# One core: whole 64-row weights ahead of the second third, the band's last quarter by GpSimd, and the loads of x5 to x9 released one by one

## The chip, the cores and the metric

The kernel runs on one core of a Trainium2 chip. The metric is the device time of one execution in microseconds. The core has TensorE (PE) for products, VectorE (DVE), ScalarE (ACT), GpSimd (POOL) and SyncE (SP), which in this kernel issues nearly all DMA transfers; in the profile "SPq" is the queue of SP.

## The reference

Per batch (8) and position (4160) a causal convolution of width 7 is taken, with one softmax-normalised set of 7 weights for each of 8 heads of 24 columns, and its result goes through a feed-forward layer with three products and a maximum.

```python
w = softmax(weight, axis=-1)                       # 8 heads x 7
out = np.einsum('hk,bskhg->bshg', w, x_unf)        # x padded by 6 rows in front
x = out.reshape(B * S, D)                          # 33280 x 192
h = np.maximum(np.maximum(x @ w1, x @ w2), x @ w3) # 192 -> 768
return (h @ w_out).astype(np.float32)              # 768 -> 192
```

## The kernel before

The 33280 rows are cut into 65 blocks of 512 (`NBLK`). All products are in 16 bits. The maximum is taken as max(x(w1-w3), x(w2-w3), 0) + x w3: `make_wd` (L320) subtracts w3 from w1 and w2, the columns' 192 rows being held as 128 rows (n = 0 and 1) and 64 rows of both (n = 2, w1 in partitions 0 to 63, w2 in 64 to 127), `top` (L508, L509) takes the maximum with ScalarE's relu and VectorE's maximum, and x w3 w_out is added with a small matrix m.

The order of the work on every engine is the order of the program; nothing is rearranged. Each engine runs its own list and waits for the others by semaphores. SP's list holds loads, stores (L684) and transposes (L429) in program order, and a transfer that waits holds up all behind it. A transfer also waits for the one eight places earlier to land, since there are eight DMA semaphores in turn.

The start: SP loads x0 and x1 (`load_x`, L167), then a third of the 128-row weights (`load_wa`, L229), the 64 rows of w3 (L244), the 64 rows of w1 and w2 for the first third of the columns (`load_wb`, L233), the second third of the 128 rows, the remaining two thirds of the 64 rows, the last third of the 128 rows, w_out, x2, x3. Meanwhile the band matrix of the convolution is built: products with shifted weights (L291) into two PSUM tiles, columns 0 to 27 and 28 to 37 of a window, from where ScalarE and VectorE copy it to four quarters of 32 partitions (L299), heads 5 to 7 first and heads 0 to 4 later. `cast_dense` (L216) turns x0 to x3 into 16 bits, and `conv_dense` (L396) multiplies them with the band; block 0's half with heads 5 to 7 goes first (`order=(1, 0)`). `l1_dense` (L544) computes the first layer of blocks 0 and 1 in parts of 128 rows ("F") and 64 rows ("H").

From block 4 on the convolution goes another way: x is loaded in halves of 39 rows by 8 pieces, GpSimd casts it (`cast_x`, L199), `conv` (L375) multiplies it, `evac` (L415) copies the result, `turn` (L429) issues two DMA transposes, and `double` (L438) lets GpSimd copy each half of the partitions to the other. The first layer (`l1`, L521) of a block reads that result. In the main loop over t, block t's first layer is interleaved with the second layer of block t-1 (`st2`, L585), the result of t-2 is stored, and the convolution of a later block stands in the middle: block 4's in block 2, 5 and 6's in block 3, 7 and 8's in block 4, and so on.

The loads of x4 to x6 stand in one piece ahead of block 0's third and fourth tile. x7 is loaded after blocks 0 and 1 are done, x8 and x9 within block 2. A load of x4 or later waits until the zeroing of its buffer (`zero_x`, L137 or L140) or the last reader of the buffer is done.

Of the kernel before, what the change touches and what calls it, by code (L numbers as in the profile page):

```python
# [15 lines left out]
P = 128  # L16
KW = 7
PAD = KW - 1
NHEAD = 8
# [4 lines left out]
HALF = P // 2  # L24
WIN = 32 + PAD
# [3 lines left out]
def kernel(  # L29
# [12 lines left out]
    nc = tc.nc  # L42
    ctx.enter_context(tc.manual_schedule())

    B, SEQ, D = x.shape
    H, KWs = weight.shape
    assert H == NHEAD and KWs == KW and D == GRP * NHEAD
    DFF = moe_w1.shape[1]
# [9 lines left out]
    for b in range(B):  # L58
        s = nfull * NBLK
        while s < SEQ:  # L60
            n = min(SEQ - s, NBLK - off)
# [24 lines left out]
    NDENSE = 4  # L86
    chunks_of = [conv_chunks(blk) for blk in blocks[:NDENSE]]
    NQ = len(chunks_of[0])
    TOK = 32
# [29 lines left out]
    xin, xbuf, XBUF, loaded = {}, [], 7, set()  # L119
# [11 lines left out]
    def zero_x(t, q0=0, q1=NR, eng=None):  # L131
# [4 lines left out]
        if eng is not None:  # L136
# [4 lines left out]
                       in_=bass.AP(tensor=zero.tensor, offset=zero.offset,  # L141
                                   ap=[list(zero.ap[0]), [0, q1 - q0], [1, D]]))

    def load_x(t, eng=nc.sync):
        if not 0 <= t < NB:
            return
        loaded.add(t)
        get_x(t)
        xf = xin[t][0]
        if t < NDENSE:  # L150
            todo = [(0, c[3], c[1] * SEQ + c[2], i) for i, c in enumerate(chunks_of[t])]
        else:
            todo = [(HALF * (i // NR) + (0 if s else LAP), KR if s else TOK,
                     b * SEQ + s - (LAP if s else 0), i % NR) for i, (b, s) in enumerate(rows_of(t))]
        parts = []
        i, n = 0, len(todo)
        row = [c[2] for c in todo]
        while i < n:
            k = i
            while k + 1 < n and todo[k + 1][:2] == todo[i][:2] and row[k + 1] - row[k] == row[i + 1] - row[i]:  # L160
                k += 1
            step = row[i + 1] - row[i] if k > i else 0
            p0, rlen, _, q0 = todo[i]
            q1 = todo[k][3] + 1
            src = bass.AP(tensor=x.tensor, offset=row[i] * D,
                          ap=[[D, rlen], [step * D, q1 - q0], [1, D]])
            eng.dma_start(out=xf[p0:p0 + rlen, q0:q1, :], in_=src)  # L167
            if parts and parts[-1][0] == rlen:
                parts[-1] = (rlen, parts[-1][1], q1)
            else:  # L170
                parts.append((rlen, q0, q1))
            i = k + 1
        xin[t] = [xf, todo[0][0], parts]
# [30 lines left out]
    xz = {t: [const.tile([P, NQ, D], FP16, name=f"xz_{t}_{v}") for v in range(2)] for t in range(2)}  # L204
    xz[2], xz[3] = xz[0], xz[1]

    def cast_dense(t, copies, slots_=range(CYC // 32), keep=False):
        xf, _, parts = xin[t] if keep else xin.pop(t)
        for v, copy in enumerate(copies):
            if copy is None:  # L210
                continue
            for s in slots_:
                cut = GRP * (32 * s // GRP + 1)
                a, b = (32 * s, cut) if v == 0 else (cut, 32 * s + 32)
                for (rl, q0, q1) in parts:
                    copy(  # L216
                        out=xz[t][v][0:rl, q0:q1, :].rearrange("p q (k c) -> p q k c", c=CYC)[:, :, :, a:b],
                        in_=xf[0:rl, q0:q1, :].rearrange("p q (k c) -> p q k c", c=CYC)[:, :, :, a:b])
# [6 lines left out]
    PW = 2 * P  # L225
# [2 lines left out]
        for st, n, wsrc in ((w3s, 0, moe_w3), (ws, 0, moe_w1), (ws, 1, moe_w2)):  # L228
            nc.sync.dma_start(out=st[:, n, f], in_=wsrc[0:P, f])  # L229

    def load_wb(f):
        for st, lo, n, wsrc in ((ws, 0, 2, moe_w1), (ws, HALF, 2, moe_w2)):
            nc.sync.dma_start(out=st[lo:lo + HALF, n, f], in_=wsrc[P:D, f])  # L233

    wk = const.tile([NHEAD, SMALL], FP32, name="wk")[:, 0:KW]
    nc.scalar.dma_start(out=wk[:], in_=weight)
# [4 lines left out]
    load_x(0)  # L241
    load_x(1)
    load_wa(slice(0, PW))
    nc.sync.dma_start(out=w3s[0:HALF, 1, :], in_=moe_w3[P:D, :])  # L244
    load_wb(slice(0, PW))
    for t in range(2, NDENSE):
        get_x(t)
    ident = const.tile([P, P], FP32)
# [32 lines left out]
    nc.vector.reciprocal(out=wrec[:], in_=wrec[:])  # L281
    zero_x(4)
    nc.vector.tensor_scalar_mul(out=line[0:NHEAD, 31:31 + KW], in0=wexp[:, 0:KW], scalar1=wrec[:])
    cast_dense(0, (nc.vector.tensor_copy, nc.gpsimd.tensor_copy), (1, 2), keep=True)
    CUT = 28
    bands_ = []
    for lo, hi, copy in ((0, CUT, nc.scalar.copy), (CUT, WIN, nc.vector.tensor_copy)):
# [5 lines left out]
                             rhs=ident16[:, 0:4 * NHEAD], start=True, stop=True)  # L293
        bands_.append((lo, hi, copy, bps))
    keep_warm((NBLK, NBLK, P), psp, "p")
    for h0, h1 in ((5, NHEAD), (0, 5)):
        for lo, hi, copy, bps in bands_:
            for a in range(4):
                copy(out=band[32 * a:32 * a + 32, h0:h1, 32 * a + lo:32 * a + hi],  # L299
                     in_=bps[:, 0:hi - lo, h0:h1].rearrange("p c h -> p h c"))  # L300
        if h0:
            cast_dense(0, (nc.vector.tensor_copy, nc.gpsimd.tensor_copy), (0,))
    load_wa(slice(PW, 2 * PW))
    load_wb(slice(PW, DFF))
    load_wa(slice(2 * PW, DFF))
    nc.sync.dma_start(out=wos[:], in_=moe_w_out.rearrange("(j p) c -> p j c", p=P))
    load_x(2)
# [76 lines left out]
    def conv_dense(t, copies, pools=((None, None),) * 2, order=(0, 1)):  # L384


        yd = dense[t] = ydp.tile([P, NC, NBLK], FP16, tag="yd", name=f"yd_{t}")
        for n in order:
            slots_ = ((0, 1, 2, 3), (4, 5, 4, 5))[n]
            pool, tag = pools[n]  # L390
            ps = (pool or psw).tile([P, NBLK], FP32, tag=tag or "w", name=f"D{n}_{t}")
            for (q, b, row_lo, rlen, lo, hi, cc) in chunks_of[t]:
                for v in range(2):
                    for g, s in enumerate(slots_):
                        h = (32 * s + 31 * v) // GRP
                        nc.tensor.matmul(  # L396
                            ps[32 * g:32 * g + 32, lo:hi],
                            lhsT=xz[t][v][0:rlen, q, 32 * s:32 * s + 32],
                            rhs=band[0:rlen, h, cc:cc + hi - lo],
                            start=(v == 0), stop=(v == 1), tile_position=(0, 32 * g))  # L400
            copies[n](out=yd[:, 2 * n, :], in_=ps[:])
# [96 lines left out]
    def meet():  # L498

        emit(True)  # L500
        assert not ops
        clock[0] = clock[1] = 0
# [189 lines left out]
    WPWQ = ((psw, "w"), (psp, "p"), (psw, "w"), (psq, "q"))  # L692
    ACT, DVE = nc.scalar.copy, nc.vector.tensor_copy
    GP = nc.gpsimd.tensor_copy
    conv_dense(0, (ACT, ACT), order=(1, 0))
    cast_dense(1, (DVE, GP), (1, 2, 0))
    zero_x(5, eng=nc.gpsimd)
    make_wd(0, 0, 2)
# [14 lines left out]
    l1_dense([(1, 0, WW), (1, 1, WW)], "HF")  # L713
    tops((1, 0), (1, 1))
    zero_x(6)
    for t in range(NDENSE, XBUF):
        load_x(t)
    l1_dense([(0, 2, PQ), (0, 3, PQ)], "FH")
    tops((0, 2), (0, 3))
    l1_dense([(1, 2, WW), (1, 3, WW)], "HF")  # L720
# [10 lines left out]
    first_hidden(0)  # L731
    first_hidden(1)
    conv_dense(2, (ACT, DVE), (WW[0], PQ[1]))
    cast_x(4)
    cross(2, ACT, DVE)
    make_m(0)
# [1 line left out]
    zero_x(0, NQ)  # L738
    zero_x(2, NQ, NR, nc.vector)
    zero_x(3, NQ, NR, nc.vector)  # L740
    load_x(7)
    cast_x(5)

    convs_at = {2: 4, 3: 5, 4: 7}
# [16 lines left out]
    for t in range(2, NB):  # L763
        u = convs_at.get(t, NB)
        late = t > 2 and u < NB
        if t in (3, 4):
            double(t + 1)
        if t > 3:
            for v in range(casts.get(t - 1, 8) + 1, casts[t] + 1):
                cast_x(v)  # L770
        l1(t, 0)
        if t == 2:
            first_rest()
        elif t == 3:
            cast_x(8)
            nc.gpsimd.tensor_copy(out=m16[0:HALF, 2, :], in_=m16[HALF:P, 0, :])
            nc.gpsimd.tensor_copy(out=m16[HALF:P, 2, :], in_=m16[HALF:P, 1, :])
        if t > 3 and not late:
            op(lambda t=t: (store(t - 2, 0, 4, (nc.sync,)),
                            turn(t + 2, (2,)) if place(t + 2)[1:] in ((0, 4), (0, 5)) else None,  # L780
                            turn(t + 1, (4,)) if place(t + 1)[1:] == (0, 5) else None, load_on(t)))
        else:
            op(lambda t=t: store(t - 2, 0, 4, (nc.sync,)))
        cuts = ROOM if late else EVEN
        st2(t - 1, (cuts[0], cuts[0]))
        for j in range(1, NJ):
            l1(t, j)
            if late and j == 1:
                st2(t - 1, (cuts[0] + OWN + AHEAD, cuts[0] + OWN))
                meet()  # L790
                quad, second = u >= QUADS, u < QUADS or t == u - 3
                conv(u, WPWQ, range(4 * second, 4 * second + 4) if quad else range(NHEAD))
                for i in (0, 2):
                    evac(u, i)
                for i in (1, 3):
                    evac(u, i, nc.vector.tensor_copy)
                if second:
                    turn(u)
                load_on(t)
            if t == 2 and j == 1:  # L800
                meet()
                conv_dense(3, (ACT, DVE))
                zero_x(1, NQ, NR, nc.vector)
                cross(3, GP, GP)
                load_x(8)
                cast_x(6)
            elif t == 2 and j == 3:
                meet()
                conv(u, WW)
                evac(u, 0)  # L810
                evac(u, 1, nc.vector.tensor_copy)
                turn(4)
                load_x(9)
                cast_x(7)
            st2(t - 1, (cuts[j], cuts[j]))
            if j == 1 and t > 4 and t + 2 in pairs and pairs[t + 2][1] % 2 == 0:
                double(t + 2)
            if t == NB - 1 and j == 3:
                op(lambda: store(NB - 2, 0, 2, (nc.sync,)))
        if t == NB - 1:  # L820
            op(lambda: store(NB - 2, 2, 4, (nc.sync,)))
# [29 lines left out]
```

## Time and profile before

| | |
|---|---|
| median of 3 runs | 454.19 us (453.32 to 454.22) |
| profiled execution | 454.16 us, its span 452.4 us |
| granted TensorE clock | 1.00 |
| TensorE busy | 445.5 us, 98% |
| VectorE, ScalarE, GpSimd busy | 354.6, 320.2, 207.6 us |
| TensorE's waits, 0 to 110 us / from 60 us | 3.8 us / none listed |
| DMA | 72.01 MB, mean 159 GB/s |

The page gives busy time by engine and the chain that ended last. A list of waits gives, for each engine and line, who ended the idle time, with the total, the number and the longest in microseconds. A timeline row gives start, duration, engine, line, operation and, in brackets, the idle time before it and what ended it. Matmul ends are modelled, and a busy TensorE is not TensorE at its peak.

### The profile page before, as it was taken

The page shows a single profiled execution, that of the slowest core. Times are in us where ns is not written, and L with a number is a line of the kernel's source. Part 1 is how long each engine was busy: PE and PEld are TensorE (multiplying, and loading weights), DVE is VectorE, ACT ScalarE, POOL GpSimd, SP SyncE. Part 2 cuts the span into 40 slices and gives each one's busy share as a digit, 9 for nine tenths or more (in the row PEclk, how much of TensorE's full clock was granted, in tenths as well). Part 3 has the DMA queues.
Part 4 walks back from the last instruction along what each step waited for, and adds up shares of the span by engine and source line. Part 5 has one row for each costly group of instructions (what it writes and reads, how often), then busy time and mean ns, then how long its engine had stood idle before and what let it go on. Part 6 is the DMA issues. An engine that isn't in the chain of part 4 may idle for free.

```text
span 452.4 us, 18264 instructions
## 1 busy us (share of the span) xinstructions
PE 445.5 (98%) x7576; PEld 409.8 (91%) x7576; DVE 354.6 (78%) x607; ACT 320.2 (71%) x601; POOL 207.6 (46%) x239
## 2 busy tenths in 40 slices
PE   7999999999999999999999999999999999999997
PEld 4469999999999989999999999999999999999996
DVE  6668787878878787787887787887887887887775
ACT  6967767767777677676676776777776776776664
POOL 5864836556463533724824635525533644224000
PEclk9999999999999999999999999999999999999999
DMA  7968987696885659649649748657649668152123
GB/s 197 239 181 167 203 186 197 155 217 171 170 220 147 165 137 205 162 121 199 167 127 198 178 110 191 191 114 193 178 112 197 172 157 143 54 136 75 58 71 106
DMA packets 128163, 72.01 MB, mean 159 GB/s; under 512 B 52305, under 2 KB 127888, under 8 KB 128080
## 3 DMA queue, kind: packets, MB, share of 16 engines
q1 hardware_dynamic: 127919, 70.75, 65.9%
q8 instruction: 59, 0.97, 0.9%
q14 instruction: 25, 0.20, 0.2%
q10 hardware_dynamic: 160, 0.10, 0.1%
HBM read 33.28 MB, written 25.56 MB: 130 GB/s over the span
## 4 chain that ended last, share of the span: by engine, by line
PE 96%; DMA 1%; ACT 1%; SPq 1%; issue 1%; DVE 0%; ACTq 0%
PE po L585 36%; PE lq L521 32%; PE lp L521 22%; PE G L375 3%; DMA wall<-in_moe_w_dram 1%; ACT r L508 1%; PE D L396 1%; PE po L643 0%; PE po L616 0%; PE lw L544 0%; SPq L229 0%; SPq L167 0%; PE pm L355 0%; ACT wall L324 0%; PE lq L544 0%
## 5 line engine op out<-in xcount | busy, mean ns | idle before, releaser
L585 PE MATMUL po<-wo,h 64*128 64x192 f16 x3024 | 331.7, 243 | 0.0
L509 DVE TENSOR_TENSOR h<-r,lq 128x512 f16<-128x512 f16 x384 | 263.0, 686 | 86.2 <-ACT r L508 76.3
L508 ACT ACTIVATE r<-lp 128x512 f16<-128x512 f32 x384 | 228.9, 597 | 113.8 <-PE lp L521 103.0
L521 PE MATMUL lp<-yp,wd 64*128 64x512 f16 x1098 | 295.6, 376 | 0.0
L521 PE MATMUL lq<-yp,wd 64*128 64x512 f16 x1098 | 295.5, 376 | 0.0
L585 PEld LDWEIGHTS <-h 64*128 64x128 f16 x3024 | 242.7, 94 | 5.4 <-issue 4.1
L521 PEld LDWEIGHTS <-wd 64*128 64x128 f16 x2268 | 181.7, 94 | 14.8 <-issue 0.2
L199 POOL CAST x<-xf 103x768 f16<-103x768 f32 x122 | 97.3, 825 | 114.4 <-DMA xf<-in_x_dram 99.6
L585 PE MATMUL po<-m,yp 64*128 64x192 f16 x720 | 140.3, 243 | 0.0
L438 POOL COPY yp<-yp 64x1536 f16<-64x1536 f16 (+1 forms) x70 | 90.9, 1298 | 86.0 <-DMA yp<-ys 49.1
L593 DVE TENSOR_TENSOR o<-a,po 128x384 f32<-128x384 f32 x126 | 69.0, 547 | 0.0
L585 PEld LDWEIGHTS <-yp 64*128 64x128 f16 x720 | 66.3, 94 | 0.1
L592 ACT COPY a<-po 128x384 f32<-128x384 f32 x126 | 59.6, 473 | 0.0
L415 ACT CAST ys<-G 128x480 f16<-128x480 f32 (+1 forms) x53 | 25.4, 530 | 9.5 <-PE G L375 9.2
L415 DVE CAST ys<-G 128x480 f16<-128x480 f32 (+1 forms) x53 | 30.1, 610 | 0.0
L375 PE MATMUL G<-x,band 39*32 39x240 f16 (+3 forms) x1024 | 16.5, 242 | 0.0
L375 PEld LDWEIGHTS <-band 39*32 39x32 f16 x1024 | 10.2, 92 | 4.6 <-issue 4.1
L521 PE MATMUL lq<-yd,wd 64*128 64x512 f16 x36 | 9.7, 376 | 0.0
L521 PE MATMUL lp<-yd,wd 64*128 64x512 f16 x36 | 9.7, 376 | 0.0
L544 PEld LDWEIGHTS <-wd 128*128 128x128 f16 (+1 forms) x48 | 3.0, 95 | 7.3 <-issue 1.7
L396 PEld LDWEIGHTS <-xz 112*32 112x32 f16 x320 | 4.1, 96 | 2.9 <-issue 1.4
L216 POOL CAST xz<-xf 112x160 f16<-112x160 f32 (+2 forms) x18 | 5.1, 328 | 3.2 <-DMA xf<-in_x_dram 3.0
(75 smaller groups left out, 100.0 us busy)
## 6 DMA issues: line engine op xcount, KB each, us to landing
xf<-in_x_dram SPq DMA_DIRECT2D x113, 234.0 KB
out_dram<-o SPq DMA_DIRECT2D x62, 384.0 KB
xf<-in_x_dram SPq DMA_DIRECT2D x7, 204.8 KB
wall<-in_moe_w_dram SPq DMA_DIRECT2D x11, 128.0 KB
xf<-in_x_dram SPq DMA_DIRECT2D x3, 420.0 KB
yp<-ys SPq DMA_TRANSPOSE x70
out_dram<-o SPq DMA_DIRECT2D x5, 192.0 KB
wos<-in_moe_w_out_dram SPq DMA_DIRECT2D x1, 576.0 KB
```

The costliest lines, as they stand in the source:

```text
L199: nc.gpsimd.tensor_copy(out=x16s[t0][0:K, :, :, u, r, :].rearrange("p h j c -> p j h c"), in_=xf[0:K, 4 * r:4 * r + 4, :].rearrange("p j ( ...
L216: copy(out=xz[t][v][0:rl, q0:q1, :].rearrange("p q (k c) -> p q k c", c=CYC)[:, :, :, a:b], in_=xf[0:rl, q0:q1, :].rearrange("p q (k c) -> ...
L375: nc.tensor.matmul(G[2 * (k // per) + i][TOK * j:TOK * (j + 1), k % per, :], lhsT=band[row, h, HALF * i + LAP:HALF * i + KR], rhs=x16s[t0] ...
L396: nc.tensor.matmul(ps[32 * g:32 * g + 32, lo:hi], lhsT=xz[t][v][0:rlen, q, 32 * s:32 * s + 32], rhs=band[0:rlen, h, cc:cc + hi - lo], star ...
L415: copy(out=slots[t][:, i % 2, :, :, GRP * h0:GRP * (h0 + per)].rearrange("p u r (h c) -> p h (u r) c", c=GRP), in_=G[i][:].rearrange("p h ...
L438: nc.gpsimd.tensor_copy(out=yp[HALF * i:HALF * (i + 1), 1, :, :, :, :].rearrange("p i u k n -> p (i u k n)"), in_=yp[HALF * (1 - i):HALF * ...
L508: nc.scalar.activation(out=r[:], in_=ps[0][:], func=AF.Relu)
L509: nc.vector.tensor_max(out=hs[t][:, j, :], in0=r[:], in1=ps[1][:])
L521: nc.tensor.matmul(ps[i][:], lhsT=w_of(i, c, j), rhs=y_all(t, i, c), start=(n == 0), stop=(n == NC - 1))
L585: nc.tensor.matmul(ps[b0, i][:, s % 2, :], lhsT=a, rhs=b, start=first, stop=last)
L592: nc.scalar.copy(out=a[:], in_=ps[s - 1, 0][:])
L593: nc.vector.tensor_add(out=outs[t][:, s - 1:s + 1, :], in0=a[:], in1=ps[s - 1, 1][:])
```

## The change

Three things are altered.

1. `load_wb` now loads the 64 rows of w3, w1 and w2 each whole (192 KB), ahead of the second third of the 128-row weights. The piece-wise loads of w1 and w2 are gone.
2. The band is copied for all heads at once, by ScalarE and VectorE for three quarters of the partitions; the fourth is copied by GpSimd from the first. x0's cast is done in one go ahead of it, and block 0's convolution takes its halves in the plain order.
3. `release_x(t)` writes one element of x_t's buffer with VectorE and then issues the load, so that the load waits for VectorE to come to that place in its list. x4 is loaded where x4 to x6 were; x5 is released after block 2's convolution, x6 ahead of block 3's, x7 after the evacuation of block 4's convolution, x8 behind the fifth step of block 2 and x9 behind the first step of block 3. The casts of x5 to x8 follow later in GpSimd's list.

```diff
+    def release_x(t):
+
+        get_x(t)
+        nc.vector.memset(xin[t][0][TOK:TOK + 1, 0, 0:1], 0.0)
+        load_x(t)
...
-    def load_wb(f):
-        for st, lo, n, wsrc in ((ws, 0, 2, moe_w1), (ws, HALF, 2, moe_w2)):
-            nc.sync.dma_start(out=st[lo:lo + HALF, n, f], in_=wsrc[P:D, f])
+    def load_wb():
+        for st, lo, n, wsrc in ((w3s, 0, 1, moe_w3), (ws, 0, 2, moe_w1), (ws, HALF, 2, moe_w2)):
+            nc.sync.dma_start(out=st[lo:lo + HALF, n, :], in_=wsrc[P:D, :])
...
     load_wa(slice(0, PW))
-    nc.sync.dma_start(out=w3s[0:HALF, 1, :], in_=moe_w3[P:D, :])
-    load_wb(slice(0, PW))
+    load_wb()
...
-    cast_dense(0, (nc.vector.tensor_copy, nc.gpsimd.tensor_copy), (1, 2), keep=True)
+    cast_dense(0, (nc.vector.tensor_copy, nc.gpsimd.tensor_copy))
...
-    for h0, h1 in ((5, NHEAD), (0, 5)):
-        for lo, hi, copy, bps in bands_:
-            for a in range(4):
-                copy(out=band[32 * a:32 * a + 32, h0:h1, 32 * a + lo:32 * a + hi],
-                     in_=bps[:, 0:hi - lo, h0:h1].rearrange("p c h -> p h c"))
-        if h0:
-            cast_dense(0, (nc.vector.tensor_copy, nc.gpsimd.tensor_copy), (0,))
+    for lo, hi, copy, bps in bands_:
+        for a in range(3):
+            copy(out=band[32 * a:32 * a + 32, :, 32 * a + lo:32 * a + hi],
+                 in_=bps[:, 0:hi - lo, :].rearrange("p c h -> p h c"))
+    nc.gpsimd.tensor_copy(out=band[96:P, :, 96:96 + WIN], in_=band[0:32, :, 0:WIN])
     load_wa(slice(PW, 2 * PW))
-    load_wb(slice(PW, DFF))
     load_wa(slice(2 * PW, DFF))
...
-    conv_dense(0, (ACT, ACT), order=(1, 0))
+    conv_dense(0, (ACT, ACT))
...
-    for t in range(NDENSE, XBUF):
-        load_x(t)
+    load_x(4)
...
     conv_dense(2, (ACT, DVE), (WW[0], PQ[1]))
+    release_x(5)
     cast_x(4)
...
-    load_x(7)
-    cast_x(5)
...
         elif t == 3:
-            cast_x(8)
+            release_x(9)
+            cast_x(7)
...
             if t == 2 and j == 1:
                 meet()
+                release_x(6)
                 conv_dense(3, (ACT, DVE))
                 zero_x(1, NQ, NR, nc.vector)
                 cross(3, GP, GP)
-                load_x(8)
-                cast_x(6)
+                cast_x(5)
             elif t == 2 and j == 3:
...
                 turn(4)
-                load_x(9)
-                cast_x(7)
+                release_x(7)
+                cast_x(6)
+            elif t == 2 and j == 5:
+                release_x(8)
+            if t == 3 and j == 3:
+                cast_x(8)
```

More of the change, by code (lines that the diff above doesn't have):

```diff
@@ L205, with cast_dense @@
     xz[2], xz[3] = xz[0], xz[1]
-    def cast_dense(t, copies, slots_=range(CYC // 32), keep=False):
-        xf, _, parts = xin[t] if keep else xin.pop(t)
+    def cast_dense(t, copies, slots_=range(CYC // 32)):
+        xf, _, parts = xin.pop(t)
         for v, copy in enumerate(copies):
```

## The prediction

> **What bounds the kernel now.** First the busy shares and the shares of the chain that ended last, from the page.
>
> ```profile
> span 452.4 us, 18264 instructions
> ...
> PE 445.5 (98%) x7576; PEld 409.8 (91%) x7576; DVE 354.6 (78%) x607; ACT 320.2 (71%) x601; POOL 207.6 (46%) x239
> ...
> PE 96%; DMA 1%; ACT 1%; SPq 1%; issue 1%; DVE 0%; ACTq 0%
> ```
>
> TensorE is the chain for 96%. Nothing that keeps it busy is touched, so the change is worth what it adds to or takes from TensorE's waits. The list of TensorE's waits in the first 110 us has them all; from 60 us on the same list is empty.
>
> ```profile
> PE idle L260 <- DVE idle L255: 1.2, 1, 1.2
> PE lp L544 <- DVE wd L320: 1.1, 1, 1.1
> PE D L396 <- issue: 0.8, 1, 0.8
> PE D L396 <- ACT band L299: 0.5, 1, 0.5
> ```
>
> The second and the third are the ones that the change can move. The chain in order of time says what they hang on.
>
> ```profile
> 3.71 6.13 DMA wall<-in_moe_w_dram
> 9.86 0.40 ACT wall L324
> ...
> 27.88 0.84 issue
> ```
>
> The early chain is a weight load; at 27.88 TensorE stands for 0.84 us in the middle of conv_dense(3) with no semaphore to wait for. Last, the timelines of SP, of GpSimd and of TensorE around the hand-over to block 5, the first place where one queue carries loads, a store and transposes whose result is wanted soon.
>
> ```profile
> 32.48 3.77 SPq L429 DMA_TRANSPOSE yp<-ys  x2
> 36.35 0.96 SPq L167 DMA_DIRECT2D xf<-in_x_dram  x2
> 37.40 0.41 SPq L684 DMA_DIRECT2D out_dram<-o  x1
> 38.34 3.05 SPq L429 DMA_TRANSPOSE yp<-ys  x2
> ```
>
> ```profile
> 44.20 2.98 POOL L438 COPY yp<-yp 64x1536 f16<-64x1536 f16 x2 [2.16 <-DMA yp<-ys]
> ```
>
> ```profile
> 44.10 0.75 PE L375 MATMUL G<-x,band 39*32 39x96 f16 x64
> ...
> 48.87 0.38 PE L521 MATMUL lp<-yp,wd 64*128 64x512 f16 x1
> ```
>
> GpSimd's double(5) waited 2.16 us for the transposes of block 5, began at 44.20 and ended at 47.18. Block 5's first product, which reads it, began at 48.87: the slack is 1.69 us.
>
> **The change part by part.**
>
> *Band and block 0's convolution.* Removed: ScalarE's eight copies (216 to 265 ns) and VectorE's eight (176 to 202). Added: three each, of 224 and 80 elements a row. From 84 elements in 216 ns and 140 in 265, 224 take about 0.34 us, so ScalarE is done at 4.71 + 1.0 = 5.7. VectorE has its three casts first (0.48 for two and 0.29, to about 5.0), then three copies of some 0.24: 5.7. GpSimd copies 304 elements behind its casts (to 5.12); 192 elements take it 0.34 us and 512 take 0.64, so about 0.45, to 5.75. The convolution starts near 5.9 instead of 5.66 and needs 1.1 us for its 80 products (conv_dense(2) at 22.21): 7.0 instead of about 7.4. It then waits for the casts of x1, which begin at 7.15 when that load lands, in both kernels. So nothing; the cover is that load, and without it the gain would be 0.4. Bounds: -0.4 and +0.2 (the later start).
>
> *Weights.* The two 64 KB pieces ahead of the second third become whole 192 KB pieces; the two 128 KB pieces later go. VectorE's third wd subtraction (10.58) needs them, then block 0's 64-row products (11.06), and behind those ScalarE's relus, which from 11.54 to 15.10 run without a break (four relus, a 1.47 us zeroing), then the products at 16.49 that wait for VectorE's h. A delay at the head passes whole. Its size: the semaphore steps in the trace show the third 128-row piece landed at 8.51, the 192 KB piece of w3 at 9.84, the two 64 KB pieces at 10.22 and 10.39. A whole piece took 1.33 us behind its predecessor on the three slowest DMA engines and 0.65 on the other thirteen; the two small ones took 0.55 together. Two whole pieces thus take 1.3 to 2.7 in place of 0.55: +0.75 to +2.1. The other way, 262 kB more at the best rate of any one-us window here (347 GB/s) is also 0.76, so no gain is possible. I take +1.0, near the thirteen engines, as the slow three had twice the others' load only while everything was saturated. In return the last third comes without the 128 KB pieces ahead of it; but GpSimd's late subtraction (waits of 1.0 us for its load at 15.47) stands behind the ScalarE chain, so that gain is 0, bound -0.4 (TensorE's pause from 16.09 to 16.49).
>
> *The stall at 27.88.* It ends without a releaser. The packet records have 16 KB code packets (the page's q8 row: 59 packets, 0.97 MB), one about every 256 TensorE instructions; the third began at 26.13, when the backlog of x4 to x6 (landed 26.98) was nearly through, and took 1.12. In the changed kernel x5 is let loose only after VectorE's copy of D_2 (24.05, later by the 1.0) and x6 after that, so the queue is empty from x4's landing (22.74 before) to about 26, and the packet comes early. I take -0.84, the whole; the other bound is 0. [...]
>
> *Loads let loose.* Each release adds a one-element memset on VectorE (0.06 us by the one of L238), in its idle gaps: 0, at most +0.06 ahead of cross(2). The loads stay as many, but on SP they move. x7, x8 and x9 now stand behind the transposes of block 4 and ahead of the store and the transposes of block 5. Before, only x9 stood there. x7's release comes at VectorE's copy of G (33.1), x8's after the fifth h (36.74), x9's after block 3's first h (37.8); SP frees at 36.3, or 35.1 if the second transpose issues in its shortest time (1.23). The issues add 2.5 us ahead of the transposes, the data more: x7 and x8 are four halves of 234 to 240 KB and one of 24 KB. At 247 and 217 GB/s (the windows 38:40 and 40:45) a half is 1.0 to 1.1 us; between semaphore completions in a queue that is full, 1.2 to 1.4 (x9's halves: 39.77, 41.20). Four halves and the small one: 4.1 to 5.6, less 0 to 1.2 for an earlier start; I take 1.15 a half, 4.8, less 0.55. So the transposes land at 44.1 + 4.25 = 48.35, double(5) runs to 51.4, and block 5 starts 2.5 us late; bounds 0 (below) and 3.9. On the way GpSimd's cast of x8 ends near 44.9 against conv(7) at 44.10: some 0.8 of the same 2.5 is lost there. Of the others, x6 lands near 32.8 and its cast ends at 34.5, 2.4 us ahead of conv(5) at 36.95; x9's cast and the next transposes have over 4 us.
>
> [...] The two pauses of TensorE here would be 2.1 and 2.5 us; the row shows a pause of 1.08 us at 10:12 with the granted clock at 1.00. [...]
>
> Sum against the profiled execution's 454.16 us (span 452.4 and 1.76 around; the median of the runs is 454.19): 0 + 1.0 - 0.84 + 2.5 = +2.66, so 456.8 us. All later blocks are moved as a whole.
>
> **The rivals.**
> - *The queue clears in time* (the other side: not slower). If the transposes of block 5 land by 48.87 - 2.98 = 45.9, block 5 starts on time, and the sum is 1.0 - 0.84 = +0.16: 454.3 us. For it: DMA was busy only 0.20 to 0.42 in 34:38, and between 28.5 and 29.5 us it began 453 packets of 768 B, against some 270 a us that I use; at that pace three loads and a store (2377 packets) take 5.2 us. Against it: with four halves ahead, at 89.15 to 96.6, the transposes landed 9.8 us after the first load's issue, and six halves would be 12.
> - *The code stall stays*, or comes back at conv(7), whose code must pass the same backlog: 457.7 us. For it: the code packet of 47.29 began 3 us after TensorE had entered its block, behind x10. Against it: that one caused no wait.
> - *A gain*: weights late by 0.75 only, stall gone, block 5 on time, and both covers gone, so that the 0.4 of the convolution and the 0.4 between 16.09 and 16.49 count: 453.3 or a little under. It needs x1 to land early and ScalarE not to be the chain; no row speaks for either.
> - *The memsets do not hold the loads*, and the change is its front part alone: excluded, as each first load half waits for VectorE in the order of the changed kernel.
>
> **How the numbers follow.** Forecast (block 5 late by 1 us or more): 0.63. The stall stays on top of it: 0.17. The queue clears, within 0.2%: 0.13. A gain: 0.07. 0.2%, 0.9 us, is about what a measurement of this kernel can tell from no change. So slower 0.63 + 0.17 = 0.80, same 0.13, faster 0.07. The range begins at 454.3, the queue that clears, which leaves out the gain and the lower half of that case, some 0.13. It ends at 459.0: with the stall kept the sum is 457.7, and the upper bounds of weights and block 5 (+1.1 and +1.4) would bring 460.2 only together.
>
> **What would show it.** Right: VectorE's third wd starts near 11.6 and the 64-row products near 12.1; no issue wait near 28; a new TensorE wait of 2 to 3 us between conv(7) and block 5's first product, released by GpSimd's L440 copy or cast, whose own releaser is the DMA of yp or xf. Wrong: transposes of block 5 landing before 46, or the 64-row products at 11.1. A surprise elsewhere would be a wait in conv(5) or at block 4.

## The result, and the profile after

The changed kernel takes 457.17 us (median of five executions, 456.59 to 458.44) against 454.19 us (452.13 to 454.66) of the kernel before on the same chip: a ratio of 1.0087, with a 95% interval from 1.0066 to 1.0107 (the two medians alone make 1.0066, the means of the listed executions 1.0082). Forecast were 456.8 us and a range from 454.3 to 459.0. The profiled execution is one of 458.13 us with a span of 456.35, so 3.97 us have to be found against the span of 452.38 before. In this document line numbers of the changed kernel are two to six higher than those of the kernel before; the kernels of the experiments have their own.

The page of the changed kernel first: busy shares, then the shares of the chain that ended last.

```profile
span 456.3 us, 18262 instructions
...
PE 447.3 (98%) x7576; PEld 408.8 (90%) x7576; DVE 354.5 (78%) x607; ACT 319.5 (70%) x596; POOL 208.3 (46%) x240
...
PE 94%; DMA 2%; SPq 1%; DVE 1%; issue 1%; POOL 0%; ACT 0%; DVEq 0%; POOLq 0%
```

TensorE's busy time went up by 1.8 us although it has the same 7576 products; that is a clock and not work, as shown below. Its waits in the first 110 us (engine, line, what ended the wait: total, number, longest) are these; from 60 us on none is listed, as before.

```profile
PE G L377 <- POOL x L205: 2.2, 1, 2.2
PE lp L546 <- DVE wd L322: 1.4, 1, 1.4
...
```

The line "issue" of 0.8 us is gone, the wait for VectorE's wd has grown from 1.1 to 1.4, and a wait of 2.2 us for GpSimd's cast stands ahead of conv(7) (L377). The chain in order of time (start, duration, who), in three places:

```profile
11.40 0.44 DVE wd L322
11.88 0.55 PE lp L546
12.43 0.42 PE lp L546
12.86 2.67 PE lw L546 x8
...
29.14 1.03 PE D L398 x69
30.18 0.52 PE po L587 x10
...
45.59 4.12 DMA yp<-ys
50.03 1.35 issue
51.38 1.48 POOL yp L440
52.90 0.37 PE lq L523
```

The 64-row products start at 11.88 instead of 11.06. In conv_dense(3) (29.14) there is no stall. Block 5 waits for GpSimd's copy, which waited for the transposes. GpSimd's timeline around conv(7) and block 5 (start, duration, line, operation; in brackets the idle time before):

```profile
45.88 1.60 POOL L205 CAST x<-xf 103x768 f16<-103x768 f32 x2 [1.06 <-DVE h L511]
49.86 2.99 POOL L440 COPY yp<-yp 64x1536 f16<-64x1536 f16 x2 [2.38 <-DMA yp<-ys]
```

The cast at 45.88 is that of x8. The releaser named there is not the one that held it: GpSimd's semaphore wait for the last part of x8 ended at 45.72, when the slowest DMA engine's step came (45.69; of the thirteen steps of that half eleven were in by 44.40 and the twelfth at 44.77). conv(7) then began at 47.53. The transposes of block 5 landed at 49.70. Of block 5 it is the first lq that waits, for the second of GpSimd's two copies; the lp ahead of it (52.29) does not.

Reading TensorE's shift against the kernel before at fixed points of the program gives the sum:

| point | before | after | shift grows by |
|---|---|---|---|
| block 0's 64-row products | 11.06 | 11.88 | +0.82 |
| first product behind the stage, po of L616/L618 | 20.30 | 22.44 | +1.32 |
| po behind conv_dense(3) | 29.08 | 30.18 | -1.04 |
| conv(7) | 44.10 | 47.53 | +2.33 |
| block 5's first lq | 49.20 | 52.90 | +0.27 |
| end | 452.38 | 456.35 | +0.27 |

Conv(5) lies between the third and the fourth row and moved from 36.95 to 38.15, which is 0.1 us more than po behind conv_dense(3). The last row is no wait that a list names: 0.13 us come near 326 us and 0.13 behind TensorE's last product. The second row, +1.32, is in no step of the prediction. The windows' view shows what it is: columns are the stretch in us, its length, TensorE's busy time with the number of products, the granted clock, the busy share of the DMA engines and GB/s.

```profile
8.57:11.98 3.41, 1.76 (x45) 1.00 0.97 272
11.98:15.39 3.41, 3.41 (x13) 0.50 0.92 282
15.39:18.80 3.41, 3.32 (x19) 1.00 1.05 251
```

From 11.98 to 15.39 us TensorE had half its clock (0.50). Two of the five executions show a mean clock of 0.996 over the span (458.13 and 458.44 us), three show 1.000 (456.59, 456.83, 457.17), 1.4 us less in the mean. All are in the comparison.

### The profile page after: what moved, and what is told of

It reads as the page before. It is cut to its first block, busy times and chain, and to the rows that moved or that the text cites. A ratio compares the mean times of both kernels' runs of the same rounds, so it can differ in the third digit from the quotient of the medians.

```text
span 456.3 us, 18262 instructions
## 1 busy us (share of the span) xinstructions
PE 447.3 (98%) x7576; PEld 408.8 (90%) x7576; DVE 354.5 (78%) x607; ACT 319.5 (70%) x596; POOL 208.3 (46%) x240
## 4 chain that ended last, share of the span: by engine, by line
PE 94%; DMA 2%; SPq 1%; DVE 1%; issue 1%; POOL 0%; ACT 0%; DVEq 0%; POOLq 0%
PE po L587 35%; PE lq L523 31%; PE lp L523 21%; PE G L377 3%; DMA wall<-in_moe_w_dram 1%; PE lw L546 1%; DMA yp<-ys 1%; PE lp L546 1%; PE D L398 0%; PE po L645 0%; PE po L618 0%; POOL yp L440 0%; SPq L235 0%; SPq L173 0%; DVE h L511 0%
## 5 line engine op out<-in xcount | busy, mean ns | idle before, releaser
L377 PE MATMUL G<-x,band 39*32 39x240 f16 (+3 forms) x1024 | 16.5, 242 | 2.2 <-POOL x L205 2.2
L377 PEld LDWEIGHTS <-band 39*32 39x32 f16 x1024 | 10.3, 91 | 6.7 <-issue 6.3
L546 PE MATMUL lw<-yd,wd 64*128 64x512 f16 (+1 forms) x24 | 6.2, 461 | 0.0
L222 POOL CAST xz<-xf 112x80 f16<-112x80 f32 (+2 forms) x18 | 5.2, 335 | 2.2 <-DMA xf<-in_x_dram 2.2
```

The costliest lines, as they stand in the source:

```text
L222: copy(out=xz[t][v][0:rl, q0:q1, :].rearrange("p q (k c) -> p q k c", c=CYC)[:, :, :, a:b], in_=xf[0:rl, q0:q1, :].rearrange("p q (k c) -> ...
L377: nc.tensor.matmul(G[2 * (k // per) + i][TOK * j:TOK * (j + 1), k % per, :], lhsT=band[row, h, HALF * i + LAP:HALF * i + KR], rhs=x16s[t0] ...
L546: nc.tensor.matmul(open_ps[t, j, i][:], lhsT=a, rhs=b, start=(t, j, i) not in begun, stop=(t, j, i) in begun)
```

## The experiments

The theory after this reading was a sum of four parts: weights late (+0.8), half clock behind the pause that they make (+1.3 in some executions), no code stall (-1.0), x7 to x9 ahead of block 5's transposes (taken as +2.8; the last three rows of the table make 2.87). Each kernel below was timed against the kernel before on the same chip, where that had a median of 453.3 to 453.5 us; differences in us are worked out from the ratios, unless medians are named. All kernels do the whole computation.

**The front alone.** Weights and band as in the changed kernel, all loads of x as before.

```diff
-            nc.sync.dma_start(out=st[lo:lo + HALF, n, f], in_=wsrc[P:D, f])
+            nc.sync.dma_start(out=st[lo:lo + HALF, n, :], in_=wsrc[P:D, :])
...
-    conv_dense(0, (ACT, ACT), order=(1, 0))
+    conv_dense(0, (ACT, ACT))
```

> The kernel before with the first two alterations alone (the 64-row weights whole, the band's last quarter by GpSimd); the loads of x4 to x9 stay where they were. Theory (the parts add up): block 0's 64-row products start near 11.9 us, +0.8; the stall near 28 us stays (0.8); block 5 is on time. So +0.8, 455.0 us, and where the half clock between 12 and 15 us comes too, as in the profiled execution of the changed kernel, +1.3 more: 456.3. Rival 1 (the half clock belongs to the loads' release, not to the front): clock 1.00 in every execution. Rival 2 (the stall near 28 us goes because TensorE comes there later, not because of the loads): no stall, 454.2.

Measured: 454.78 us, ratio 1.0024 (1.0010 to 1.0038), so +1.1 us. Two of twelve executions had the clock of 0.996, the profiled one among them (span 453.6): rival 1 fell, the half clock belongs to the front too. Its 64-row products start at 12.01, and then:

```profile
8.78:12.20 3.42, 1.67 (x29) 1.00 0.91 230
12.20:15.61 3.41, 3.41 (x13) 0.50 0.95 298
```

The stall is gone in this execution although the loads of x4 to x6 are where they were. The 16 KB packet of code came at the same time as before (25.92 to 27.10), but TensorE, 2.2 us later, had not yet come to what it holds. The span says the same: 0.95 for the later products, 1.3 for the clock and 0.84 less for the stall make +1.4, and it is 1.2 longer than before. So in this execution the delay of the front itself swallowed the stall, which I had counted to the release alone; that is rival 2's condition. An execution of it with the full clock was not profiled. The ten with the full clock have a mean of 454.50 us, 0.9 above that of the kernel before, which fits the theory's +0.8 with the stall kept and not rival 2's 0; that the front takes away the stall there too is not shown.

**The release alone.** The front as before, x5 to x9 let loose as in the changed kernel.

```diff
-    for t in range(NDENSE, XBUF):
-        load_x(t)
+    load_x(4)
...
+    release_x(5)
     cast_x(4)
...
+            elif t == 2 and j == 5:
+                release_x(8)
```

> The kernel before with the third alteration alone (x5 to x9 let loose one by one). Theory: the 64-row products of block 0 stay at 11.06, the stall near 28 us goes (-0.8 to -1.0), conv(7) waits some 2.3 us for GpSimd's cast of x8, block 5 another 0.5 for its transposes: +1.8 to +2.0, 456.1 us, clock 1.00 in all. Rival (the 0.8 us by which the front is late pushes the loads and the casts into each other, so that without it the queue clears earlier): waits at conv(7) and block 5 under 1 us in all, 454.2 or less.

Measured: 455.94 us, ratio 1.0069 (1.0043 to 1.0095), +3.1 us. With the front's 0.24% the two parts make 0.93%, and the whole change 0.87%: the parts add up within their intervals, and three quarters of the loss are the release. The waits of the profiled execution, and the rows of conv(5) and conv(7) in TensorE's timeline:

```profile
PE G L381 <- POOL x L205: 1.6, 2, 1.3
...
PE lq L527 <- POOL yp L444: 0.9, 1, 0.9
PE G L381 <- issue: 0.6, 1, 0.6
```

```profile
37.60 0.75 PE L381 MATMUL G<-x,band 39*32 39x96 f16 x64 [1.34 <-POOL x L205]
...
45.04 0.50 PE L381 MATMUL G<-x,band 39*32 39x96 f16 x39 [0.22 <-POOL x L205]
```

The place was expected wrongly. The long wait, 1.3 us, is at conv(5) and for the cast of x6, whose last steps came at 35.70 to 35.80; conv(7) waits 0.2 us and not 2.3. x8's cast ran from 43.39 and ended at 44.98. Nothing of x8 was late. GpSimd could begin x7's cast only when x7 had landed (40.51), and behind it in its list stand two copies of m, a memset and the cast of x8, 4.3 us in all. The rival's waits (under 1 us at conv(7) and block 5 together) were nearly met, with 1.15 us; its time was not. Two executions of nine had the clock of 0.996 (459.46 and 458.97 us), without the new front; so the front is not needed for the lower clock. They lie 3.4 us above the mean of the other seven. One stretch of 3.41 us at 0.50, as in the changed kernel's trace, would cost 1.7 at most by estimate: in these two something else was longer too, which no profile shows. And there is a stall without a releaser in the middle of conv(7):

```profile
45.04 0.50 PE G L381 x39
45.54 0.56 issue
46.10 0.34 PE G L381 x25
```

**x6 alone.** Only the load of x6 is moved behind block 2's convolution.

```diff
-    for t in range(NDENSE, XBUF):
+    for t in range(NDENSE, XBUF - 1):
         load_x(t)
...
+    release_x(6)
     cast_x(4)
```

> The kernel before, with only the load of x6 let loose behind block 2's convolution; x4, x5 stay ahead of block 0's third tile, x7 to x9 where they were. Theory (the stall near 28 us is instruction code that is held up behind the backlog of x4 to x6): with x6 gone from the backlog the code packet comes through early, the stall goes, nothing else moves: -0.8 to -1.0, 453.3 us. Rival 1 (the stall isn't from the backlog): it stays, 454.2. Rival 2 (x6 then delays x7's load and the transposes of block 4): no stall, but a new wait at block 4 or conv(5), 454.2 or more.

Measured: 453.93 us, ratio 1.0009 (0.9992 to 1.0026): no gain shown. The theory's expectation of -0.8 fell, and so did rival 1. The stall near 28 us is gone and a new one stands elsewhere:

```profile
PE po L591 <- issue: 1.1, 1, 1.1
```

In TensorE's list (a weight load and a product each time, 7576 of each in the trace, its few semaphore instructions left out) the stall of the kernel before stands ahead of instruction 960. This one stands ahead of instruction 1216, which is 256 later, and the stall inside conv(7) of the kernel with the release alone ahead of 1726, three times 256 later but for two.

**x7 to x9 early.** The changed kernel with x7, x8 and x9 loaded where the kernel before loads them.

```diff
+    load_x(7)
...
-            release_x(9)
...
+                load_x(8)
                 cast_x(5)
...
-                release_x(7)
+                load_x(9)
                 cast_x(6)
-            elif t == 2 and j == 5:
-                release_x(8)
```

> The changed kernel with the loads of x7, x8 and x9 issued where the kernel before issues them; x5 and x6 stay let loose, weights and band stay altered. Theory (the waits at conv(7) and block 5 come from x7 to x9 standing ahead of block 5's transposes): both waits go, -2.8 against the changed kernel: 454.0 us at full clock (+0.8 for the weights, -1.0 for the stall), 455.3 with the half clock. Rival (x5 and x6, now late, push x7 to x9 as far back by themselves): waits of 1 to 2 us stay at conv(7) or block 5, 455.5 or more at full clock.

Measured: 455.94 us, ratio 1.0059 (1.0038 to 1.0081), +2.7 us. The expectation of -2.8 against the changed kernel fell, the rival came nearer. The chain of the profiled execution (span 453.6; only one execution of seven was faster) shows where:

```profile
28.80 5.86 DMA xf<-in_x_dram
34.81 1.61 POOL x L205 x2
36.46 0.74 PE G L377 x64
...
37.83 0.52 issue
...
43.16 1.60 POOL x L205 x2
44.80 0.74 PE G L377 x64
```

x6, let loose late and now behind x7, landed so late that its cast (34.81) holds conv(5) by 0.5 us; then another stall of 0.52 us without a releaser, ahead of instruction 1470; and x8's cast again ends just as conv(7) begins. The limit had moved from one load to the next.

**Products of zeros in the pause.** The changed kernel, with something for TensorE to do ahead of the 64-row products.

```diff
+    keep_warm((NBLK,) * 6, psw, "w")
     l1_dense([(0, 0, PQ), (0, 1, PQ)], "H")
```

> The changed kernel with six more products of zeros (512 columns each, into a PSUM tile that nobody reads) in TensorE's pause ahead of block 0's 64-row products, about 1.3 us of work in a pause of 1.4 us. Theory (the pause and the light convolution products before it bring the half clock from 12 to 15 us): the clock is 1.00 in that stretch in every execution, the executions at 0.996 are gone, and the median is that of the undisturbed executions of the changed kernel, +2.6 against the kernel before. Rival 1 (the half clock comes from the pause of 2.2 us at conv(7)): executions at 0.996 stay, as in the kernel with the loads' release alone, where 2 of 9 had it. Rival 2 (the products cost time because the pause is shorter in most executions): +3.5 or more.

Measured: 457.1 us, ratio 1.0083 (1.0059 to 1.0107), and two of six executions still at 0.996: rival 1. The +3.8 us are in rival 2's range as well, and the four executions with the full clock have a mean of 456.76, against 456.86 of the changed kernel's three: nothing gained, and no price of the products that shows. In the profiled execution the clock between 10 and 17 us is 1.00 throughout, as the theory had it. But behind the pause at conv(7) it is not:

```profile
43.83:47.24 3.41, 1.34 (x79) 1.00 1.01 181
47.24:50.65 3.41, 3.41 (x29) 0.50 1.24 230
```

So the half clock has two places. What stood ahead of it, and where it stayed away, is in the last section.

**Code moved by 40 instructions.** The kernel before with twenty more products of zeros, small ones, in the same pause.

```diff
+    keep_warm((HALF // 2,) * 20, psw, "w")
     l1_dense([(0, 0, PQ), (0, 1, PQ)], "H")
```

> The kernel before with twenty more products of zeros of 32 columns in TensorE's pause ahead of block 0's 64-row products: they move TensorE's later instructions 40 places down its list (a product is two instructions) and leave everything else alone. Theory (TensorE's stall is a 16 KB piece of its instruction list that begins at instruction 960 = 3 x 256 + 192 and comes late): the stall still ends near 28.7 us, but now stands ahead of the 46th product of conv_dense(3) instead of the 66th, so it is longer by twenty products of 13.8 ns: +0.3, 454.0 to 454.5 us. Rival (the stall belongs to the data or the PSUM of that convolution): it stays ahead of the 66th or 67th product with 0.8 us, and the time is that of the kernel before.

Measured: 454.54 us, ratio 1.0030 (1.0017 to 1.0043), +1.4 us. The place is as the theory had it: the stall stands ahead of weight load 480 as before, but that is now the 46th of conv_dense(3), twenty products earlier. The chain shows it at 0.66 us behind the first product of that convolution, where in a second profile of the kernel before it comes at 0.89 us:

```profile
26.64 0.66 PE D L396 x38
27.30 0.54 issue
...
30.65 0.58 PE G L375 x61
31.23 1.16 issue
```

The expected size was wrong. That stall is shorter (0.54 us, the packet came 0.8 us earlier), and the next one, at instruction 1216, now costs 1.16 us: TensorE now needed that piece at 31.2 us, and its packet came no sooner than before (29.92 against 29.96). The rival, that the stall is tied to the convolution's data, fell.

**Half of x6.** The kernel before with only the second of x6's two loads let loose behind block 2's convolution.

```diff
-    for t in range(NDENSE, XBUF):
+    for t in range(NDENSE, XBUF - 1):
         load_x(t)
+    load_half(6, 0)
...
+    release_half(6, 1)
     cast_x(4)
```

> The kernel before with only the second half of x6 let loose behind block 2's convolution, the rest of the loads where it was. Theory (each 16 KB piece of TensorE's code queues behind the loads that are under way when it is asked for; letting loose all of x6 only handed the stall on from instruction 960 to 1216): half as much moved frees the third piece by 1.2 us, where 0.84 was missing, and delays the fourth by less than its slack of some 0.8 us, so neither stalls: -0.6 to -0.8, 453.5 us. Rival (the wait is not proportional to the backlog): a stall of 0.4 us or more stays at 960 or at 1216, and the time is that of the kernel before within 0.3 us.

Measured: 453.16 us, ratio 0.9992 (0.9983 to 1.0002). The profile has no stall and a span of 451.4 us; its waits are these.

```profile
...
PE lp L563 <- DVE wd L339: 0.6, 1, 0.6
PE lq L563 <- DVE h L528: 0.2, 1, 0.2
```

In this execution neither piece stalls, as the theory had it; the gain is not there: 0.2 us by the medians, 0.4 by the ratio, not told apart from none. What did change is the spread: its eleven executions lie between 452.94 and 453.28 us, those of the kernel before on that chip between 452.45 and 454.74.

**x6 and x7.** x6 let loose behind block 2's convolution, x7 loaded right ahead of x8.

```diff
+    release_x(6)
     cast_x(4)
...
-    load_x(7)
     cast_x(5)
...
+                load_x(7)
                 load_x(8)
```

> The kernel before with x6 let loose behind block 2's convolution and x7 loaded behind block 3's, right ahead of x8. Theory: both pieces of code come through (no stall at 960 or 1216), the transposes of block 4 land some 1.5 us later, at 38.9 against a limit of 39.1 less the 0.84 gained, so block 4 waits 0.5 us or less: -0.3 to -0.8, 453.6 us. Rival 1: the transposes come later than that and block 4 waits 1 us or more: 454.5 or more. Rival 2: the fifth piece of code (needed at instruction 1472) is now the one behind the loads: a stall of 0.5 to 1 us there, 454.2.

Measured: 453.14 us, ratio 0.9996 (0.9984 to 1.0007): no difference. Rival 2 has it: pieces three and four come through, and the next does not. The stall of 0.6 us stands ahead of instruction 1472.

```profile
36.42 0.18 PE lp L527
36.60 0.59 issue
37.20 0.24 PE po L591
```

**Weights in pieces.** The changed kernel with the 64-row weights loaded as before; it differs from the release alone only by the band.

```diff
     load_wa(slice(PW, 2 * PW))
+    load_wb(slice(PW, DFF))
     load_wa(slice(2 * PW, DFF))
```

> The changed kernel with the 64-row weights loaded in pieces as before (two thirds of w1 and w2 behind the second third of the 128 rows); the band by GpSimd and the loads' release stay. Theory (the front's loss is the weights' alone): block 0's 64-row products start at 10.5 to 11.2 us instead of 11.9, no half clock between 12 and 15 us, and the time is that of the kernel with the loads' release alone, +2.6 to +3.1 against the kernel before. Rival (the band's last quarter by GpSimd costs by itself, as its wait of 0.4 to 0.8 us ahead of block 0's convolution suggests): +3.5 or more, the time of the changed kernel.

Measured: 455.99 us, ratio 1.0062 (1.0037 to 1.0087), +2.8 us. That is the release alone (1.0069) and less than the whole change (1.0087), though the intervals overlap. Its 64-row products start at 10.70. So the band is worth nothing that shows, and the front's loss goes with the weights as far as these intervals tell. Two of nine executions were at 0.996 here too, as with the release alone; that the half clock would be gone was expected of the front's stretch, where the profiled execution has 1.00, and cannot be said of the others.

**x7 early.** The changed kernel with x7 alone at its old place.

```diff
     zero_x(3, NQ, NR, nc.vector)
+    load_x(7)
...
-                release_x(7)
                 cast_x(6)
```

> The changed kernel with x7 alone loaded where the kernel before loads it; x5, x6, x8, x9 stay let loose. Theory (what stands ahead of block 5's transposes is paid by the half, at 1.15 us each): two halves fewer, so x8's last half lands near 43.4 instead of 45.7 and the transposes at 47.4 instead of 49.7; conv(7) waits 0 to 0.5 us instead of 2.2, block 5 not at all: -2.2 to -2.7 against the changed kernel, +1.5 against the kernel before; up to 0.7 more if x6, now behind x7, is late for conv(5). Rival (the queue is held up by something else, as SP's own pace or the store): the wait at conv(7) stays over 1.2 us.

Measured: 455.47 us, ratio 1.0039 (1.0027 to 1.0050), +1.8 us: 2.2 us less than the changed kernel by the ratios, as expected. x8's last step came at 43.4 us and the transposes landed at 47.2, both as forecast. The wait at conv(7) is 0.9 us instead of the expected 0 to 0.5, block 5 does not wait, and conv(5) waits 0.4 for x6. So the price by the half holds in this direction. Some 0.3 of the 2.2 us may be the clock: two of twelve executions had 0.996, against two of five of the changed kernel, at 1.4 us each.

**x9 behind the transposes.** The changed kernel with x9 loaded after the transposes of block 5.

```diff
-    loads.update({2: 9, 3: 10})
+    loads.update({2: 8, 3: 10})
...
-            release_x(9)
```

> The changed kernel with x9 loaded behind the transposes of block 5 instead of ahead of them; x5 to x8 stay let loose. Theory (conv(7)'s wait and block 5's are two waits with two loads behind them): the wait of 2.2 us at conv(7) stays, since x8 doesn't pass x9; the transposes of block 5 land 2.3 us earlier and block 5's wait of 0.4 us goes: -0.4 to -0.5 against the changed kernel. Rival 1 (one wait, of the queue as a whole): conv(7)'s wait shrinks too, -1.5 or more. Rival 2 (x9 and block 6's transposes are late in turn): a new wait of 0.5 us or more at block 6 or conv(9), no gain.

Measured: 457.21 us, ratio 1.0071 (1.0050 to 1.0091), with three of six executions at 0.996. Block 5's wait is gone (transposes landed at 46.1, 3.6 us earlier), as the theory had it. The wait at conv(7) is 0.8 us here, which looks like rival 1, but the front of that execution was 0.3 us later still, had the half clock too, and x8's cast was held by GpSimd's list and not by x8. A new stall of 0.6 us without a releaser stands at 60.3 us, in a later convolution. Against the changed kernel the gain of 0.16% is smaller than the intervals: not settled by this run.

**The kernel before, once more.** No edit; for its profile on the chip of the last three runs above and of most of the others.

> The kernel before once more, for its profile on the chip of these runs, where its median is 453.3 us and not 454.2. Theory (the stall of TensorE near 28 us is a late piece of code, and how late is a matter of the single execution): the stall is under 0.5 us or absent here, which would be why the kernel that lets loose half of x6, without any stall, is only 0.2 us ahead. Rival (the stall is the same 0.8 us): then something else in that kernel takes back what the stall gave.

Measured: 454.65 us, and a stall of 1.31 us, longer than the 0.84 of the first profile. The expectation, under 0.5 us or none on this chip, fell for this execution.

```profile
27.01 0.89 PE D L396 x57
27.90 1.31 issue
29.21 0.36 PE D L396 x15
```

It is one of the slower executions of the kernel before, 1.5 us of span above the kernel with half of x6 (profiled on another chip), of which 1.3 are the stall. What the faster executions of the kernel before look like was not seen; that the stall varies from one to the next would explain both the spread and the missing gain, but is argued, not shown; this one profile, from the slow end, does not decide it.

## Why the prediction was right, and where it was not

*Band and block 0's convolution, forecast 0.* Right: the convolution starts at 5.89 (forecast 5.9) and then waits for x1. In the front alone GpSimd's copy held it until 6.52, and block 1's convolution began no later for it (7.49). The kernels with and without the new band, all else equal, are at 1.0062 and 1.0069.

*Weights, forecast +1.0.* Mis-sized a little: VectorE's third subtraction 11.40 (forecast 11.6), the products +0.82. Over the profiles with the old order of weights the products start at 10.44 to 11.24, with the new order at 11.07 to 12.20 (without the kernels that have products of zeros there), so the means differ by 0.87 and a single execution says little.

*The stall, forecast -0.84.* Right as to what it is, as far as the runs show it, a piece of TensorE's code held up by the loads: with 40 instructions put in ahead it still stood ahead of instruction 960, and with x6 alone let loose it was gone from there. The measured gain is 1.04. In the release alone the packet began at 23.77 instead of 26.12, as the step had it. But the step counted it to the release of the loads alone; the front alone was without it in the profiled execution too, since TensorE came later. And the forecast's rival "comes back at conv(7)" is what the release alone showed (0.56 us inside conv(7)), though not the changed kernel's own profile. With x6 alone, x6 and x7, x7 to x9 early and the release alone a stall of 0.5 to 1.1 us stood further on, ahead of instructions 1216, 1472, 1470 and 1726; the changed kernel's own profile and that with half of x6 have none.

*Loads let loose, forecast +2.5, of it 0.8 at conv(7).* The sum is right, 2.33 + 0.27 = 2.60; the split is not. The term that failed is the time of x8's cast: forecast to end at 44.9, it ended at 47.48. In the release alone and with the weights in pieces it did end at 44.98 and 44.90. In the profiled execution of the change all of this was 1.0 us later than forecast, with the clock, which moves conv(7) as much and so explains no wait. Of the 1.4 us that are left (2.2 less the forecast's 0.8) the last DMA engine explains 1.05: its share of x8 came 1.3 us behind eleven others, and without it GpSimd's list would have let the cast begin at 44.83 instead of 45.88. This is worked out from the one trace, not tested. The transposes of block 5 landed at 49.70 (forecast 48.35), and since TensorE was then 2.3 us late already, block 5 waited only 0.27 more. The slack there was also 0.33 us larger than the prediction counted: what needs the second copy is the first lq (49.20 before), not the lp at 48.87. It is one queue that sets both, but two waits on the path, and the larger one is the earlier.

*x6, forecast to land near 32.8 and to be cast by 34.5, 2.4 us ahead of conv(5).* Wrong, and covered by luck. Its last seven steps came together at 36.25 to 36.34, with block 4's transposes under way; what held them is not shown. The cast ended at 38.09 and conv(5) began at 38.15, so the wait was 0.1 us because TensorE was 1.1 us late. Where TensorE came earlier, conv(5) waits: 1.3 us in the release alone, 0.6 with products of zeros, 0.5 with the weights in pieces. So the loss of the release is fairly steady and its place is not.

*The pauses cost nothing, forecast from a row with a pause of 1.08 us.* This is the step that failed, +1.32 us in the profiled execution: the half clock delayed the products by 1.6 us up to 15.33, and 0.3 of that was taken up by pauses of the kernel before, above all by its fifth wait, 0.2 us for VectorE's h at 16.49, which the prediction's list does not show. The prediction went by that row, where the clock stayed at 1.00; here the pause of 1.40 us up to 11.88 was followed by 3.41 us at 0.50 from 11.98.

*Rivals.* That the queue clears in time was seen in no kernel that lets x7 to x9 loose ahead of block 5's transposes. The gain was seen nowhere. In sum the forecast had the sign, the stage and the two main prices; it is 1.3 us short of the profiled execution, and that is the clock. The other rows of the table make 2.65 against the forecast's 2.66; that they agree so closely is luck, since each term is off by 0.1 to 0.3.

## What to carry to other kernels

A load that is moved later must be followed to every queue that it then shares: here to GpSimd's list behind it, to the transposes on SP's queue and to the code of TensorE, whose third packet began at 23.77 us in the release alone and at 26.12 in the kernel before. When a stall has no releaser, count the instructions ahead of it: here it stood ahead of instruction 960 also when 40 instructions were put in ahead of it, and five kernels that moved loads had one of 0.5 to 1.1 us further on instead. Read the granted clock behind a pause of TensorE too, and not the length of the pause alone: in the profiled execution of the changed kernel 1.4 us of pause, in a stretch of 3.41 us with 1.76 us of products, were followed by 3.41 us at 0.50, and TensorE's shift grew by 1.32 us more.

## What was not expected of the hardware

*The half clock and the busy time ahead of it.* In the traces of these kernels the granted clock changed only at points that lie a whole number of 3.41 us from the first clock record (5.15 and 11.98 in the changed kernel, 6.27 and 47.23 with products of zeros, 6.45 and 13.28 with x9 behind), and where these points fall differs from execution to execution. Stretches taken from these points can be read in pairs, TensorE's busy time in one and the clock in the next. With x9 behind, then x7 early, then x7 to x9 early, then the changed kernel at its pause of 2.2 us ahead of conv(7):

```profile
9.86:13.28 3.42, 1.47 (x11) 1.00 0.79 233
13.28:16.69 3.41, 3.41 (x10) 0.50 0.95 283
```

```profile
10.01:13.43 3.42, 1.85 (x13) 1.00 0.68 195
13.43:16.84 3.41, 3.29 (x18) 1.00 1.08 313
```

```profile
7.76:11.17 3.41, 1.96 (x69) 1.00 1.04 282
11.17:14.58 3.41, 3.28 (x20) 1.00 0.87 268
```

```profile
46.11:49.52 3.41, 1.99 (x85) 1.00 1.07 205
```

Busy times of 1.34, 1.47, 1.67 and 1.76 us of 3.41 were followed by half the clock (0.50) for 3.41 us; 1.85, 1.96 and 1.99 were not. One stretch falls out of this order, at the end of the front alone:

```profile
449.10:452.52 3.42, 1.48 (x18) 1.00 0.51 173
452.52:453.60 1.08, 0.00 (x0) 1.00 0.00 0
```

At the same place 1.28 us with the code moved were followed by half the clock. TensorE's busy time is modelled, and what makes the clock change is not shown by these stretches. The changed kernel's long pause at conv(7) fell across two stretches, with 2.66 and 1.99 us of products, and the clock stayed at 1.00; its short pause fell into one that was thin anyway, 1.76 us, with the products of block 0's convolution and its casts. Mean clocks of 0.996 came in 17 of the 66 executions of the changed kernel and of those that keep the new weights or let x8 loose, in one of the 12 with the code moved, in one of the 76 of the kernel before that ran beside them, and in none of the 35 of the three that only move x6 or x6 and x7.

*Where code stalls.* The nine stalls of 0.5 us or more without a releaser after the first 12 us stand ahead of TensorE's instructions 960 (three times), 1216 (twice), 1470 and 1472, 1726 and 2236 (x9 behind): 256, 510, 512, 766 and 1276 behind the first place, which is whole steps of 256 within four. With TensorE's semaphore instructions ahead of them counted too (two to five), the steps hold within one. Each ended 1.3 to 1.7 us after the end of a 16 KB packet of the instruction queue (28.72 against 27.24 in the kernel before). In eleven profiles the packet of the third piece began when TensorE was at instruction 754 to 766, some 200 ahead of the need; in the three with the backlog of x4 to x6 and the old front it began at 820 to 836. The kernel before and the changed kernel have 59 such packets for 15152 weight loads and products each; no profile has more than two stalls of this size.
